# Expert ranks by triangular products, and expert 0's first products written into the last attention blocks

## The chip, the cores and the metric

The kernel runs on one core of one Trainium2 chip. The metric is the time of one execution on the device in microseconds; three executions are known, and a fourth was profiled. TensorE (PE) multiplies; VectorE (DVE), ScalarE (ACT) and GpSimd (POOL) do the elementwise work; SyncE (SP) issues the loads, GpSimd the scatters.

## The reference

A sliding-window attention with sink tokens is followed by a mixture of experts with a sticky top-1 gate. Four batches, 8 heads, 768 positions, head size 64; 8 experts, 512 to 1024 to 512.

```python
scores = q @ k.T / sqrt(D)                     # keep: key < n_sink (4) or 0 <= row - col < window (128)
a = softmax(where(keep, scores, -1e9)); x = (a @ v), heads side by side      # [B, S, 512]
for s in range(S):                             # the sticky gate, per batch
    fresh_e = argmax(x[b, s] @ w_gate)
    e = fresh_e if s == 0 or sigmoid(x[b, s] @ w_local) < 0.5 else prev_e
    prev_e = e
    out[b, s] = softmax(logits)[e] * (relu(x[b, s] @ w1[e]) @ w2[e])
```

## The kernel before

All products are in float32 made of two reduced parts: a high part h, a low part l, and the three products h·h, h·l, l·h.

**Attention.** 8 groups (4 batches, two halves of the heads) of 6 blocks of 128 rows: 48 blocks, in the loop `for n in range(nb + 3)` in `attention`. It is a pipeline written out by hand: iteration n issues the scores of block n (`score`, L548), turns block n-1 (`turn`, L578, copied by ScalarE at L585), applies block n-2 to v (`apply`, L609 and L614, into tile av), and finishes block n-3 (`collect` L500, `back` L504 into bank bk, `finish` L520 and L524). The mask step L560 on VectorE makes the row maximum and ScalarE takes the exponential (L563). Each engine works through its own list in this order; a wait at one instruction holds all that stand behind it on that engine. Tiles of tag "b" (bk, and the small PSUM tiles of the routing) share one bank.

**Routing.** When the last block of a batch is finished, `routing` is put on a list, and `step()` runs one piece of it per iteration, as the tables STEPS and ENDING say. A piece reduces the gate logits (L248), finds the expert (L252 to L266, ends with fk: fresh expert, and whether the token sticks), turns fk on PE (`turn`, L280, tile tf), and runs the sticky gate along the tokens as a scan on VectorE over 8 partitions (`stay`, L285). Then `count` finds a token's rank among those of its expert: a second scan (L291, running counts ct, carried from batch to batch in `run`) and a product (L293), per half of 384 tokens. PE brings expert, slot base and rank back to rows (tile tm, L326, `base_r`), VectorE makes slots and chances (L332 to L339), and GpSimd scatters the token rows into the buffer xs at their slots (L342), one transfer per block.

**Between.** The last batch is routed in two parts, blocks 0 to 2 (`LAST`) in the branch, blocks 3 to 5 after it. Meanwhile ScalarE and GpSimd split expert 0's first weights into w_a (`first_high` L446, `first_low` L450), and two blocks of rows of expert 0 that earlier batches have scattered are read back and turned (`early_rows`, `early_prep`, tile xpfe).

**Experts.** After the branch a planner (`Agenda`, with due times by estimated product time) mixes `ffn` of expert 0's early 256 rows (first products L1000 into h_s, second products L1049 into the two `late` banks), the tail's routing, `counts`, the loads of the next rows (`lead`, xrsn, L934), and the split of w_b (expert 0's second weights, L879 by ScalarE, L880 by VectorE or GpSimd). Then each expert runs an arm of a switch, chosen by its number of rows (`tc.Switch`); `between` issues the late second products while the switch jumps. In expert 0's arm (the rest of its rows, 64 at a time of 128 columns in this data: L991) four chunks of expert 1's first weights are split into w_c, as SHORT says: ScalarE casts (L879), GpSimd or VectorE subtracts (L880).

Of the kernel before, what the change touches and what calls it, by code (L numbers as in the profile page):

```python
# [43 lines left out]
MERGE = 7  # L44
WARM = 12
# [12 lines left out]
NSM = NBLK * E + NBLK + B * NBLK + 10  # L58
# [8 lines left out]
def kernel(ctx, tc, qkd, vn, vs, w1, w2, nw, c_misc, c_ident, c_idw, c_small,  # L67
# [12 lines left out]
    xs = dram.tile([E * CAP, ROW], F32, name="xs")  # L80

# [149 lines left out]
    base_r = rt.tile([40, 10], F32R, name="base_r")

    def setup():
        nc.sync.dma_start(xs[0:P, :], zrow)
        nc.gpsimd.tensor_copy(identb, ident)
        nc.scalar.copy(base_r, base_f)

    def routing(b, i0, i1, sfx, ps, ptag, apart=False):
        n = f"{sfx}{b}_{i0}"
        nb, q0, q1 = i1 - i0, i0 * P, i1 * P  # L240
        nq = nb * P
        xb, lw, orr = xb_t[b % 2], lw_t[b % 2], orr_t[b % 2]

        def tile(nm, *shape, dt=F32, bufs=1):
            return rt.tile([P, NBLK, *shape], dt, tag=nm, bufs=bufs, name=f"{nm}{n}")[:, 0:nb]
# [3 lines left out]
        if apart:  # L249
            yield  # L250
# [6 lines left out]
        nc.vector.tensor_reduce(out=m2, in_=eq, axis=AX.X, op=ALU.max)  # L257
        nc.vector.scalar_tensor_tensor(out=fr, in0=lg[:, :, E], scalar=-1.5 * 2.0 ** -23,
                                       in1=first[:, i0:i1], op0=ALU.is_lt, op1=ALU.max)
        if apart:  # L260
            yield
        fk = fk_t[:, 0:nb]
# [4 lines left out]
        if not apart:  # L267
            yield
# [32 lines left out]
        if apart:  # L301
            chances()
# [996 lines left out]
```

## Time and profile before

| what | us |
|---|---|
| three runs | 599.86, 602.12 (median), 609.26 |
| the profiled execution: time, span | 606.81, 605.0 |
| first scores to last scores (47 blocks) | 5.98 to 224.78 |
| last scores to expert 0's arm | 224.78 to 284.39 |
| expert 0's arm | 284.39 to 304.86 |
| experts 1 to 7 | 313.31 to 605.0 |

Mean granted TensorE clock 0.925. A row of the order of time has start, length, engine, line, operation, output<-inputs, shapes and count, and in brackets the idle time before it and what ended it. A row by stretches has start:end and length, then for each of the five engines its busy time and count, then the granted clock, the share of the DMA engines and GB/s.

### The profile page before, as it was taken

The page shows a single profiled execution, that of the slowest core. Times are in us where ns is not written, and L with a number is a line of the kernel's source. Part 1 is how long each engine was busy: PE and PEld are TensorE (multiplying, and loading weights), DVE is VectorE, ACT ScalarE, POOL GpSimd, SP SyncE. Part 2 cuts the span into 40 slices and gives each one's busy share as a digit, 9 for nine tenths or more (in the row PEclk, how much of TensorE's full clock was granted, in tenths as well). Part 3 has the DMA queues.
Part 4 walks back from the last instruction along what each step waited for, and adds up shares of the span by engine and source line. Part 5 has one row for each costly group of instructions (what it writes and reads, how often), then busy time and mean ns, then how long its engine had stood idle before and what let it go on. Part 6 is the DMA issues. An engine that isn't in the chain of part 4 may idle for free. (4 is left out here: it accounts for less than half of the span.)

```text
span 605.0 us, 11792 instructions
## 1 busy us (share of the span) xinstructions
PE 541.8 (90%) x3896; PEld 458.8 (76%) x3896; DVE 354.4 (59%) x1288; ACT 284.9 (47%) x850; POOL 233.3 (39%) x188
## 2 busy tenths in 40 slices
PE   6899997989788886779589999989999899999995
PEld 3688786768667765668579978887887679888894
DVE  5677887587758865563736627464454866272321
ACT  2788785578548574222426318161532636132220
POOL 4973370837181064132616106253440355302201
PEclk7699998899799898579679999999999999999999
DMA  8633403252234034138148027484632719211000
GB/s 298 254 105 127 168 12 157 89 186 91 74 137 162 1 117 164 59 106 260 62 117 284 37 74 262 142 282 126 255 122 64 264 66 343 77 39 38 36 22 34
DMA packets 30473, 80.38 MB, mean 133 GB/s; under 512 B 3774, under 2 KB 5310, under 8 KB 30272
## 3 DMA queue, kind: packets, MB, share of 16 engines
q1 hardware_dynamic: 25520, 65.41, 31.4%
q0 software_dynamic: 4176, 12.64, 5.5%
q14 instruction: 148, 1.21, 0.7%
q8 instruction: 53, 0.87, 0.7%
q10 hardware_dynamic: 576, 0.25, 0.1%
HBM read 63.27 MB, written 16.06 MB: 131 GB/s over the span
## 5 line engine op out<-in xcount | busy, mean ns | idle before, releaser
L563 ACT ACTIVATE pef<-smf,biasf 128x264 f32<-128x264 f32 (+2 forms) x192 | 93.6, 489 | 58.8 <-DVE biasf L560 58.8
L560 DVE CUSTOM_DVE_ANT_0 smf<-sf,mask 128x264 f32<-128x264 f32 (+2 forms) x192 | 66.8, 402 | 14.6 <-PE sf L548 7.9
L1011 ACT ACTIVATE hx<-h 128x256 fp32r<-128x256 f32 (+3 forms) x72 | 24.2, 359 | 107.4 <-PE h L1000 91.7
L1049 PE MATMUL late<-w_a,hx 128*128 128x512 f32 (+2 forms) x288 | 68.8, 393 | 1.0 <-issue 1.0
L979 DVE SCALAR_TENSOR_TENSOR hx<-h,hx 128x256 fp32r<-128x256 f32 (+3 forms) x72 | 26.7, 390 | 70.2 <-ACT hx L1011 66.1
L1049 PEld LDWEIGHTS late<-w_a,hx 128*128 128x128 f32 (+2 forms) x288 | 50.7, 179 | 14.5 <-issue 1.5
L578 PE MATMUL tpf<-ident,pef 128*128 128x128 f32 x352 | 56.3, 300 | 2.2 <-ACT ptf L585 2.0
L1049 PE MATMUL late<-w_b,hx 128*128 128x512 f32 (+1 forms) x216 | 55.7, 415 | 2.3 <-DMA xs<-zrun 2.0
L1031 POOL DMA_INDIRECT out_dram<-ot_d,oi_d x18 | 18.7, 1037 | 100.4 <-DVE ot_d L1030 80.2
L614 PE MATMUL avf<-ptf,v 128*64 128x128 f32 x704 | 54.1, 294 | 1.6 <-issue 1.6
L1049 PEld LDWEIGHTS late<-w_b,hx 128*128 128x128 f32 (+1 forms) x216 | 41.6, 196 | 14.0 <-ACT w_b L879 2.1
L585 ACT COPY ptf<-tpf 128x512 f32<-128x512 f32 (+1 forms) x96 | 51.1, 532 | 1.0 <-issue 0.5
L578 PEld LDWEIGHTS tpf<-ident,pef 128*128 128x128 f32 x352 | 40.9, 150 | 12.4 <-ACT ptf L585 5.4
L1011 ACT ACTIVATE hx<-hs 128x96 fp32r<-128x96 f32 (+2 forms) x72 | 16.7, 274 | 70.6 <-DVE hs L994 59.5
L614 PEld LDWEIGHTS avf<-ptf,v 128*64 128x64 f32 x704 | 40.7, 145 | 7.7 <-issue 3.2
L520 DVE TENSOR_TENSOR xb<-bkf,rsf 128x256 f32<-128x256 f32 x48 | 20.3, 423 | 36.4 <-ACT ptsf L595 28.1
L504 PE MATMUL bkf<-idw,xtf 128*128 128x146 f32 x192 | 35.8, 311 | 5.2 <-DVE xtf L500 2.3
L880 POOL TENSOR_TENSOR w_c<-raw,w_c 128x1024 fp32r<-128x1024 f32 x11 | 27.9, 2543 | 31.6 <-ACT w_c L879 26.2
L342 POOL DMA_INDIRECT xs<-xb,slotf x21 | 20.5, 976 | 50.9 <-DVE early_i L362 31.8
L880 POOL TENSOR_TENSOR w_b<-raw,w_b 128x1024 fp32r<-128x1024 f32 x10 | 25.6, 2556 | 36.3 <-ACT w_b L879 27.8
L880 POOL TENSOR_TENSOR w_a<-raw,w_a 128x1024 fp32r<-128x1024 f32 x10 | 26.5, 2650 | 30.2 <-ACT w_a L879 28.1
L548 PE MATMUL sf<-w_a 64*128 64x264 f32 (+2 forms) x288 | 29.2, 325 | 8.3 <-DVE biasf L560 2.2
(228 smaller groups left out, 1146.2 us busy)
## 6 DMA issues: line engine op xcount, KB each, us to landing
raw<-in_dram SPq DMA_DIRECT2D x53, 512.0 KB, 6.0
raw<-in_dram SPq DMA_DIRECT2D x14, 800.0 KB
xr_0n<-xs SPq DMA_DIRECT2D x21, 258.0 KB, 2.7
v<-in_dram SPq DMA_DIRECT2D x7, 768.0 KB, 8.4
raw_w<-in_dram SPq DMA_DIRECT2D x7, 512.0 KB
raw<-in_dram SPq DMA_DIRECT2D x10, 256.0 KB
xs<-zrun SPq DMA_DIRECT2D x9, 258.0 KB
xr_0r<-xs SPq DMA_DIRECT2D x8, 258.0 KB, 3.1
```

Source lines behind the costliest of these rows:

```text
L342: s_i = nc.gpsimd.indirect_dma_start(out=xs[:, :], out_offset=bass.IndirectOffsetOnAxis(ap=slot[:, j:j + 1].bitcast(U32), axis=0), in_=xb[ ...
L504: mm = nc.tensor.matmul(bk[:, pr * WX:(pr + 1) * WX], blk["xt"][:, pr, :], idw[:, g * NPR + pr, :], start=True, stop=True, skip_group_chec ...
L548: u["mm"] = nc.tensor.matmul(sps[:, t, :w], qx[ROWS[t], i * P:(i + 1) * P], kx[ROWS[t], off:off + w], start=m == 0, stop=m == 2)
L560: u["dve"] = nc.vector.tensor_tensor_reduce(out=sm[:, :w], in0=sps[:, t, :w], in1=mk, scale=-0.125, scalar=BIG, op0=ALU.add, op1=ALU.min, ...
L563: nc.scalar.activation(pe[:, h, :w], sm[:, :w], AF.Exp, bias=bias[:, t:t + 1], scale=-1.0, accum_out=z[:, h, 0:1])
L578: nc.tensor.transpose(tp[:, t, k, :], pe[:, 2 * c + t, o:o + P], ident)
L585: nc.scalar.copy(pt[:, :, 0:nt, :], tp[:, :, 0:nt, :])
L614: nc.tensor.matmul(avt[ROWS[t], pr, :], prep["v"][:, j, 2 * pr + t, :], x["pt"][:, t, k, :], start=i < 2 and pr == 0 and k == 0, stop=pr = ...
L880: todo += [lambda s=s: lo(out=l[:, s], in0=raw[:, s], in1=h.bitcast(F32)[:, s], op=ALU.subtract) for s in ([slice(0, FF)] if eng[1] == "po ...
L979: nc.vector.scalar_tensor_tensor(out=d[:, :, 1, :], in0=h, scalar=0.0, in1=d.bitcast(F32)[:, :, 0, :], op0=ALU.max, op1=ALU.subtract)
L1011: relu = nc.scalar.activation(d[:, :, 0, :], h, AF.Relu)
L1049: nc.tensor.matmul(o, a, w, start=t == 0, stop=t == len(mm) - 1, skip_group_check=half)
```

## The change

**Ranks.** The count scans (L291, L293) and `run` go. The experts of all tokens stay as one-hot rows in `ohs` (bf16, made by ScalarE from tm), with the sum over earlier blocks in `cum`. A token's slot is now three kinds of products in one PSUM tile rk: a strictly upper triangle times its own block, ones times the blocks ahead of it in the batch, ones times `cum`, and the slot base. The steps have other tables: pieces 2 and 3 run in one iteration, the second half's scan gets an iteration of its own, tm comes at iteration 9 of 12, rk at 10, slots and scatters at 11.

TensorE, in the fourth group of the loop, around the selection of the first batch; sf are scores, tpf turns, bkf back, avf apply. Before:

```order
L578 MATMUL tpf_1_3_1_1728<-ident,pef_1_3_0_1625 128x128 x4
L589 MATMUL bkf_1733<-ident,pkf_1713 96x128
L504 MATMUL bkf_1733<-idw,xtf_1715 128x146 x2
L609 MATMUL avf_1755<-ptsf_1668,srf_1_1401 128x128 x2
L614 MATMUL avf_1755<-ptf_1_2_0_1666,v_80 64x128 x4
L614 MATMUL avf_1755<-ptf_1_2_1_1676,v_80 64x128 x4
L326 MATMUL tmf_0_1769<-base_r,orr_151 128x10 x6
L548 MATMUL sf_1_5_0_1780<-qk_b 128x264 x6
```

Now:

```order
L670 MATMUL avf_1695<-ptf_1_1_1_1621,v_85 64x128 x4
L321 MATMUL tmf_0_1704<-base_r,orr_155 128x8 x6
L604 MATMUL sf_1_4_0_1719<-hq 128x264 x6
...
L670 MATMUL avf_1776<-ptf_1_2_1_1687,v_85 64x128 x4
L336 LDWEIGHTS identb
L336 MATMUL rkf_0_1787<-ohs,identb 128x48
L336 LDWEIGHTS onesb
L336 MATMUL rkf_0_1787<-cum,onesb 128x48
L336 MATMUL rkf_0_1787<-base_r 128x48
L336 LDWEIGHTS onesb
L336 MATMUL rkf_0_1787<-ohs,onesb 128x40
```

The selection moved one iteration ahead, and eight rank products (five with ohs and ones, the last three not shown) stand behind the next apply, ahead of the scores of block 5. (The triangle's tile shares a buffer with identb, whose name the row shows.)

**The last blocks.** The loop ends after 48 iterations. What was iterations 48 to 50, the routing of the last batch (both parts), the counts and the eight first products of expert 0's early rows (`early_first`, 12 products each, into four two-bank tiles and the banks a and b) is written out in one list. `first_high` and `first_low` run an iteration earlier, and first for the half of the columns that the first four products read. TensorE's list from the turn of block 47 on, before:

```order
L578 MATMUL tpf_1_5_1_3682<-ident,pef_1_5_0_3596 128x128 x4
L589 MATMUL bkf_3687<-ident,pkf_3673 96x128
L504 MATMUL bkf_3687<-idw,xtf_3675 128x146 x2
...
L280 MATMUL tff_0_0_3733<-identb,fk 8x128
L504 MATMUL bkf_3743<-idw,xtf_3741 128x146 x2
...
L504 MATMUL bkf_3762<-idw,xtf_3760 128x146 x2
L326 MATMUL tmf_0_3770<-base_r,orr_152 128x10 x3
L384 MATMUL xpfe_3789<-ident,xr_164 128x128 x4
L384 MATMUL xpfe_3798<-ident,xr_165 128x128 x4
L834 UNCONDITIONAL_BRANCH
```

Now (he are expert 0's first products):

```order
L634 MATMUL tpf_1_5_1_3735<-ident,pef_1_5_0_3637 128x128 x4
...
L449 MATMUL hef_3782<-x_a,w_a 128x256 x12
...
L560 MATMUL bkf_2_3814<-idw,xtf_1_3810 128x146 x2
L449 MATMUL hef_3782<-x_a,w_a 128x256 x12
...
L449 MATMUL hef_3849<-x_a,w_a 128x256 x12
L321 MATMUL tmf_0_3873<-base_r,orr_156 128x8 x3
L449 MATMUL hef_3849<-x_a,w_a 128x256 x12
...
L449 MATMUL hef_3986<-x_a,w_a 128x256 x12
L449 MATMUL hef_4002<-x_a,w_a 128x256 x24
L985 UNCONDITIONAL_BRANCH
```

The rows of expert 0 are turned ahead of block 47, the first products fill the list between the small steps of the routing, and none is left behind the branch.

**After the branch.** No planner: 8 casts of w_b by ScalarE, 8 subtractions by VectorE, the 32 products with high weights (both late banks in turn, f by f), the rows' turns, then the 16 with low weights. Two chunks of expert 1's first weights are split here, the other two in expert 0's arm, both by GpSimd. VectorE in that arm, before and now (64 rows):

```order
L994 TENSOR_REDUCE hs_1_0_1_11625<-h_1_0_1_11616 128x64
L979 SCALAR_TENSOR_TENSOR hx<-hs_1_0_0_11610,hx 128x64
L880 TENSOR_TENSOR w_c<-raw,w_c 128x512 x2
L994 TENSOR_REDUCE hs_1_0_2_11652<-h_1_0_2_11643 128x64
L979 SCALAR_TENSOR_TENSOR hx<-hs_1_0_1_11625,hx 128x64
```
```order
L1114 TENSOR_REDUCE hs_1_0_1_11875<-h_1_0_1_11866 128x64
L1099 SCALAR_TENSOR_TENSOR hq<-hs_1_0_0_11860,hq 128x64
L1114 TENSOR_REDUCE hs_1_0_2_11896<-h_1_0_2_11887 128x64
L1099 SCALAR_TENSOR_TENSOR hq<-hs_1_0_1_11875,hq 128x64
L1145 COPY oi_1_d_11901<-xm_61 128x1
```

VectorE has no subtraction of weights there any more. The tile hx lies now where the keys of the odd groups lay (hq).

The diff, cut to its core:

```diff
-STEPS = {2: 1, 3: 1, 4: 1, 5: 1, 9: 1, 10: 1, 11: 2}
-ENDING = {38: 1, 39: 1, 40: 1, 41: 1, 42: 1, 43: 1, 44: 2, 45: 1, 47: 1, 48: 2, 49: 1, 50: 2}
+STEPS = {2: 1, 3: 2, 4: 1, 5: 1, 9: 1, 10: 1, 11: 2}
+ENDING = {38: 1, 39: 2, 40: 1, 41: 1, 42: 1, 43: 1, 44: 2, 45: 1, 46: 2}
-FIRST = 0, 2, 1, 3, 4, 6, 5, 7
+FIRST = 0, 2, 4, 6, 1, 3, 5, 7
...
-        def count(h):
-            w, c = len(parts[h]) * P, h * hb * P
-            o = oh[:, q0 + c:q0 + c + w]
-            nc.vector.tensor_tensor_scan(ct[:, c:c + w], ones8.broadcast_to([E, w]), o, ct[:, c - 1:c] if c else run,
-                                         ALU.mult, ALU.add)
-            nc.vector.tensor_tensor(out=orr[32:40, q0 + c:q0 + c + w], in0=ct[:, c:c + w], in1=o, op=ALU.mult)
...
+        tm = ps.tile([P, NBLK, E], F32, tag=ptag, name=f"tm{n}")[:, 0:nb]
         for j in range(nb):
+            nc.tensor.matmul(tm[:, j, :], orr[:, q0 + j * P:q0 + (j + 1) * P], eye_r, start=True, stop=True)
+        oh_k = ohs[:, k0:k0 + nb]
+        nc.scalar.copy(oh_k, tm)
...
+        rk = ps.tile([P, NBLK, E], F32, tag=ptag, name=f"rk{n}")[:, 0:nb]
+        mm = [(rk, trib, oh_k), (rk, onesb, cum.unsqueeze(1).broadcast_to([P, nb, E])),
+              (rk, ones_r, cap_r.unsqueeze(1).broadcast_to([E, nb, E]))]
+        for j in range(nb - 1):
+            mm.append((rk[:, j + 1:nb], onesb, oh_k[:, j:j + 1].broadcast_to([P, nb - 1 - j, E])))
+        for x, (o, w, m) in enumerate(mm):
+            nc.tensor.matmul(o, w, m, start=x == 0, stop=x == len(mm) - 1, skip_group_check=True)
...
+    def early_first(f, hs):
+        h1, l1 = w1_of(0)
+        mm = [(w, a, k) for k in range(KC) for w, a in ((h1, 0), (h1, 1), (l1, 0))]
+        for t, (w, a, k) in enumerate(mm):
+            nc.tensor.matmul(hs, w[:, k, f * P:(f + 1) * P], early_x[0][:, k, a, :n_e], start=t == 0,
+                             stop=t == len(mm) - 1)
+        d = hx[:, f, 0:2 * n_e].rearrange("p (j a c) -> p j a c", a=2, c=P)
+        nc.scalar.activation(d[:, :, 0, :], h, AF.Relu)
...
-                for n in range(nb + 3):
+                for n in range(nb):
...
+                apply(z, f"{nm}_0")
+                collect(z[0]["blk"], f"{nm}_0")
+                next(head_r)
+                next(head_r)
+                first_steps(0)
+                apply(a, f"{nm}_1")
...
+                next(tail_r)
+                first_steps(3)
...
+                low_steps(2)
+                counts(ps_t, "t")
...
+                first_steps(5)
+                low_steps(2)
+                first_steps(6, 7)
+                low_steps(4)
...
+    with tc.manual_schedule(engines=set(ORDERED)):
         for c in range(3):
             w_load(NCH + c)
+        for c in range(KC):
+            h, l = h2(2 * c, 2), l2(2 * c, 2)
+            second_high(second_raw[c], h)
+            for s in halves:
+                last_low = nc.vector.tensor_tensor(out=l[:, s], in0=second_raw[c][:, s], in1=h.bitcast(F32)[:, s],
+                                                   op=ALU.subtract)
+        for f in range(FC):
+            for j in (1, 0):
+                for a in range(2):
+                    late_product(f, j, a, h2, start=f + a == 0)
...
-    SHORT = (("act", "pool"), ("act", "dve"), ("act", "pool"), ("act", "pool"))
+    SHORT = (("act", "pool"),)
...
+    for c in range(2):
+        h, l = [t[:, c, :] for t in w1_of(1)]
+        second_high(raw_t[c], h)
+        i = nc.gpsimd.tensor_tensor(out=l, in0=raw_t[c], in1=h.bitcast(F32), op=ALU.subtract)
...
+    for j in range(2):
+        preps[j][0]()
+    for f in range(FC):
+        late_product(f, 1, 0, l2, stop=f == FC - 1)
+    for j in range(2):
+        preps[j][1]()
+    preps[2][0]()
+    for f in range(FC):
+        late_product(f, 0, 0, l2, stop=f == FC - 1)
+    preps[2][1]()
+    store_late(1, "_0")
```

More of the change, by code (lines that the diff above doesn't have):

```diff
@@ L57 @@
 MISC = N2 + SK
[L58 removed]
+NBASE = 2 * E + P
+NSM = NBLK * E + NBLK + B * NBLK + NBASE + P
 NX = HG * SK * 3
@@ L301, in routing @@
-        if apart:
-            chances()
-        turn(0)
-        if apart:
-            yield
-        for h in range(1, len(parts)):
-            turn(h)
-            stay(h - 1)
-            if apart:
-                yield
-        if not apart:
-            chances()
-            yield
-        stay(len(parts) - 1)
-        if not apart:
-            yield
-        for h in range(len(parts)):
-            if apart and h == len(parts) - 1:
-                yield
-            count(h)
-        nc.vector.tensor_copy(run, ct[:, nq - 1:nq])
@@ new lines, in routing @@
+        if not direct:
+            rp, rk = rk, tile("rks", E)
+            nc.scalar.copy(rk, rp)
+        yield
+        slot = tile("slot", dt=I32, bufs=2)
+        sl = tile("sl", E)
+        nc.vector.tensor_tensor(out=sl, in0=rk, in1=oh_k, op=ALU.mult)
+        nc.vector.tensor_tensor(out=ex, in0=ex, in1=oh_k, op=ALU.mult)
+        with nc.allow_low_precision(reason="one of eight summands is not zero, an integer below 2^15"):
+            nc.vector.tensor_reduce(out=slot, in_=sl, axis=AX.X, op=ALU.add)
@@ L801, in attention, with bank, ending @@
                     step()
-                for _ in early_prep(sfx, ps_s, "s"):
-                    pass
+                y, z, a = blocks[nb - 3:]
+                b, g = B - 1, G - 1
+                nm = f"{sfx}{nb}"
+                def bank(k):
+                    return ps_t.tile([P, 512], F32, tag="t", name=f"bk{nm}_{k}")
+                def ending(blk, i, bk):
+                    finish(b, g, i, blk, bk, nm)
+                (high0, low0), (high1, low1) = early_prep(sfx, ps_s, "s")
@@ new lines, in attention @@
+                bk = bank(1)
+                back(g, z[0]["blk"], bk)
+                collect(a[0]["blk"], f"{nm}_1")
+                ending(z[0]["blk"], NBLK - 2, bk)
+                bk = bank(2)
+                back(g, a[0]["blk"], bk)
+                next(head_r)
+                ending(a[0]["blk"], NBLK - 1, bk)
+                next(tail_r)
+                first_steps(1)
+                next(head_r)
+                first_steps(2)
+                next(head_r)
+                next(tail_r)
@@ L823, in attention @@
                 free.append(True)
-                pend.append(early_prep(sfx, ps_s, "s"))
+                while pend:
+                    step()
                 first_load(range(2 * KC))
@@ L830, in attention @@
                     second_load(c)
-            while pend:
-                step()
+                for high, low in early_prep(sfx, ps_s, "s"):
+                    high()
+                    low()
+                counts(ps_m, m_tag)
+                masked()
+                for f in range(FC):
+                    early_first(f, ps_s.tile([P, 2, 512], F32, tag="s", name=f"he{sfx}{f}")[:, 0, 0:n_e])()
     with tc.If(narrow != 0) as branch:
```

344 lines of the change are left out of this document (197 added, 147 removed).

## The prediction

> **What bounds the kernel now.** I read the summary first (PE busy 90% of the span, every other engine under 60%), then cut the span by the groups of the attention loop, then read TensorE's order of time wherever a stretch was longer than its like. These are busy times by stretch; the times at the left are the first scores of groups 1 to 7, then the last scores, the end of the branch, expert 0's arm, and experts 1 to 7.
>
> ```profile
> core 0: us, PE busy (x) PEld busy (x) DVE busy (x) ACT busy (x) POOL busy (x), PEclk, DMA share, GB/s
> 35.21:56.57 21.36, 21.36 (x242) 18.56 (x241) 16.50 (x86) 17.73 (x65) 11.86 (x11) 1.00 0.32 120
> 56.57:81.46 24.89, 22.89 (x255) 19.24 (x253) 20.19 (x101) 20.43 (x71) 11.93 (x11) 1.00 0.27 103
> 81.46:111.45 29.99, 26.93 (x248) 23.12 (x246) 22.40 (x94) 19.29 (x67) 13.51 (x12) 0.83 0.23 86
> 111.45:139.39 27.94, 24.10 (x255) 19.47 (x253) 20.42 (x104) 19.26 (x67) 15.84 (x18) 1.00 0.41 149
> 139.39:169.39 30.00, 26.79 (x248) 23.02 (x246) 22.43 (x94) 19.37 (x67) 13.51 (x12) 0.83 0.26 87
> 169.39:198.02 28.63, 24.37 (x255) 19.64 (x253) 20.24 (x104) 19.06 (x66) 11.94 (x14) 1.00 0.42 154
> 198.02:224.78 26.76, 22.71 (x206) 18.61 (x205) 18.24 (x84) 16.16 (x54) 7.32 (x8) 0.87 0.16 61
> 224.78:248.57 23.79, 14.85 (x120) 12.01 (x118) 14.72 (x64) 10.75 (x30) 10.82 (x10) 0.76 0.39 127
> 248.57:284.39 35.82, 31.95 (x169) 27.67 (x170) 17.32 (x63) 9.31 (x21) 9.36 (x6) 0.83 0.44 145
> 284.39:304.86 20.47, 13.13 (x77) 11.85 (x77) 15.39 (x33) 7.78 (x20) 9.69 (x5) 0.68 0.27 88
> 313.31:605.00 291.69, 277.39 (x1624) 240.12 (x1624) 143.47 (x369) 106.06 (x267) 92.96 (x52) 0.99 0.39 134
> ```
>
> Group 1, without routing, takes 21.36 us and PE is always busy: the loop is PE's at full clock. The others are 3.5 to 8.6 us longer, and groups 3 and 5, where tokens are counted, run at a mean clock of 0.83. From the last scores to expert 0's arm (59.6 us) PE is busy 46.8 us at clocks of 0.76 and 0.83, and in expert 0's arm 13.1 of 20.5 us at 0.68. Experts 1 to 7 (291.7 us) have PE busy at 0.99, and the change hardly touches them. So three stretches can give something.
>
> **Ranks in the loop.** In group 3 the counting step stands on VectorE ahead of work that PE needs. TensorE (groups 2 and 3; tff is the same kind of step where nothing is counted), then VectorE, then the clock (the third number from the right):
>
> ```profile
> 76.69 0.54 PE L280 MATMUL tff<-identb,fk 128*8 128x128 bf16 x6 [1.63 <-ACT ptf L585]
> ...
> 81.03 0.50 PE L280 MATMUL tff<-identb,fk 128*8 128x128 bf16 x6
> ...
> 94.32 1.09 PE L614 MATMUL avf<-ptf,v 128*64 128x128 f32 x16
> ...
> 99.24 0.28 PE L589 MATMUL bkf<-ident,pkf 128*96 128x128 f32 x1 [1.71 <-DVE pkf L568]
> ...
> 104.34 0.37 PE L326 MATMUL tmf<-base_r,orr 40*128 40x10 f32 x1 [0.82 <-DVE orr L293]
> ```
> ```profile
> 95.94 0.28 DVE L599 TENSOR_TENSOR ptsf<-bkf,ptsf 32x128 fp32r<-32x128 f32 x1
> 96.35 0.97 DVE L285 TENSOR_TENSOR_SCAN orr<-kff,orr 8x384 fp32r<-8x384 bf16 x1
> 97.25 0.98 DVE L291 TENSOR_TENSOR_SCAN ctf<-ones,zrun,orr 8x384 f32<-8x384 f32 x1
> 98.27 0.55 DVE L293 TENSOR_TENSOR orr<-ctf,orr 8x384 fp32r<-8x384 f32 x1
> ```
> ```profile
> 101.00:110.00 9.00, 7.73 (x48) 6.90 (x44) 4.76 (x19) 4.32 (x17) 4.08 (x4) 0.50 0.00 0
> 261.55:264.26 2.71, 2.71 (x14) 2.71 (x14) 1.94 (x16) 0.10 (x1) 1.40 (x2) 0.50 0.06 23
> ```
>
> Each half of a batch costs a count scan and a product, 0.98 + 0.55 = 1.5 us of VectorE, once ahead of pkf (PE waits 1.71) and once ahead of tm (PE waits 0.82 for the fourth of six products). Then the clock is at 0.50 for nine microseconds. All of this goes. In its place the selection products (tm) stand an iteration later than the last scan, so that wait is gone, and eight rank products (rk) stand an iteration after these. Both write bank b, which VectorE gives free with the last reader of bk, L599 in this fence: it ends at 96.22, PE's apply at 95.41. I charge each of the two stops this lag, 0.8, and its products. The trace has no rank products: 0.083 each as tff (0.50 for 6 bf16 products at full clock) is the lower bound, 0.37 as tm at half clock the upper; eight are 0.7 to 3.0. I take 0.9, since they are bf16 with small outputs as tff. So two stops are 3.5; with 1.4 for the new reductions and the scan left over, groups 3 and 5 come to 21.4 + 4.9 = 26.3: **−3.7 each**. Groups 2, 4 and 6 get the second scan (0.97) that stood in the next group, **+0.9 each**; steps 2 and 3 now follow each other in one iteration: the wait of 1.63 for fk grows by step 2's five small ops to some 2.6, and pkf is no longer delayed by these an iteration before, no difference. In group 7 the counting goes, but three small products of expert 0's row count and flags wait there: **−1.4**. Sum −7.4 + 2.7 − 1.4 = **−6**; from −12 (all stops hidden) to +8 (three more clock drops at 4.5, below).
>
> **The last blocks and the branch's end.** TensorE again, and what two of its products cost at full clock:
>
> ```profile
> 228.17 1.09 PE L614 MATMUL avf<-ptf,v 128*64 128x128 f32 x16
> ...
> 235.00 0.53 PE L280 MATMUL tff<-identb,fk 128*8 128x128 bf16 x6 [1.44 <-DVE fk L265]
> ...
> 243.32 0.77 PE L326 MATMUL tmf<-base_r,orr 40*128 40x10 f32 x3 [2.21 <-DVE orr L293]
> ...
> 248.57 5.46 PE L1000 MATMUL h_s<-x_a,w_a 128*128 128x256 f32 x24 [2.57 <-issue]
> ...
> 260.65 0.49 PE L326 MATMUL tms<-base_r,orr 40*128 40x10 f32 x3 [1.66 <-DVE orr L293]
> ...
> 281.51 1.03 PE L384 MATMUL xpsn<-ident,xrsn 128*128 128x128 f32 x8
> ...
> 313.31 11.54 PE L1000 MATMUL h<-x_a,w_c 128*128 128x256 f32 x96 [0.59 <-DMA out_dram<-ot_d,oi_d]
> ...
> 328.26 8.46 PE L1049 MATMUL late<-w_a,hx 128*128 128x512 f32 x36
> ```
>
> PE ends block 45's apply at 229.3 and then walks from wait to wait. The changed list puts expert 0's 96 products (11.54 in group 313.31, at full clock) into these waits. From 229.3: 16 transposes 2.1; the two applies left, 16 products in 1.09 and two sink products, 2.6; three banks of sink and back products at about 0.4, an estimate from the same row, 1.3; 96 products 11.5; 12 tff 1.0; 20 small ones (tm, rk, counts) at 0.1, 2.0; waits that stay (the last exponentials, both scans; an estimate) 1.7: 22.2, so PE leaves the branch at 251.5. VectorE keeps up: its list there is shorter by the two count scans. The jump costs 2.6 (the 2.57 of issue), the first cast of w_b 0.6 (no PE work covers it). Then 32 high products at 8.46/36 = 0.235 are 7.5, 1.7 more because a gap of 3.2 will have halved the clock; 12 transposes 1.5; 16 low products 3.8; 0.5 for a bank of x_b: 270.1 against 284.4, **−14.3**. The lower bound of the gain is −8: the lows run on VectorE now, and rows can come late. These are POOL's and SP's rows:
>
> ```profile
> 265.11 0.96 POOL L342 DMA_INDIRECT xs<-xb,slots  x1 [0.30 <-issue]
> 269.06 1.79 SPq L934 DMA_DIRECT2D xrsn<-xs x3
> xrsn<-xs SPq DMA_DIRECT2D x3, 258.0 KB, 4.4
> ```
>
> SP's loads start 3.0 after the last scatter and land 4.4 later. The tail's rank products stand ahead of expert 0's last three (3 × 12 products, 4.3, before 251.5); with the counts on VectorE between, the slots come at about 249, three scatters (0.96, some 0.3 apart) end at 253, rows are there at 260 to 262, and PE wants them at 263.8: just hidden; SP has only the pad and weight loads ahead of them. The upper bound is −20 (no halved clock, no waits).
>
> **Expert 0's arm.** VectorE, then ScalarE and GpSimd:
>
> ```profile
> 291.11 3.45 DVE L880 TENSOR_TENSOR w_c<-raw,w_c 128x512 fp32r<-128x512 f32 x2 [1.73 <-ACT w_c L879]
> 294.69 2.17 DVE L979 SCALAR_TENSOR_TENSOR hx<-hs,hx 128x64 fp32r<-128x64 f32 x1
> 298.22 3.13 DVE L979 SCALAR_TENSOR_TENSOR hx<-hs,hx 128x64 fp32r<-128x64 f32 x1
> 301.67 0.21 DVE L979 SCALAR_TENSOR_TENSOR hx<-hs,hx 128x64 fp32r<-128x64 f32 x1
> ```
> ```profile
> 290.48 3.20 ACT L879 CAST w_c<-raw 128x512 fp32r<-128x512 f32 x6
> 291.50 5.28 POOL L880 TENSOR_TENSOR w_c<-raw,w_c 128x1024 fp32r<-128x1024 f32 x2 [3.71 <-ACT w_c L879]
> ```
>
> Four chunks of expert 1's weights are split inside this short arm, and VectorE's ops stretch whenever GpSimd splits (2.17 and 3.13 for one that takes 0.21). Two chunks move ahead of the arm, under the late products, and the two that stay go to GpSimd: VectorE loses 3.45, ScalarE four of its casts, 4 × 3.20/6 = 2.1. I keep both stretched ops: **−5.6**; from −9 (they go too) to 0. [...]
>
> **Sum.** −6.0 − 14.3 − 5.6 = −25.9. The profiled execution has a span of 605.0 and a time of 606.8: 579.1 and 580.9. It is 4.7 above the median of the runs shown, 602.1; predicted for the median is **576 us**.
>
> **Rivals.** (1) Expert 0's arm is GpSimd's. Its two chunks (2.6 each) start only when ScalarE has cast them, the rows come late, and the arm keeps its 20.5 while the end of the branch gives 10: 602 − 6 − 10 = 586. For it: GpSimd is the last to finish in that arm now; against: one chunk fewer and none on VectorE. (2) More than I count: the two products hide in VectorE's lag, the clock stays whole, and the stretched ops go: −12 − 18 − 9, 563. (3) **The slower side**: the clock. PE now stops at fk, tm and rk in three batches and at two small products in group 7: 11 places. A drop costs what 101 to 110 shows, 9 us at half clock, about 4.5. A gap of 1.63 (76.69) did not drop the clock, 1.66 (260.65) did at once, the 0.50 of 261.55. My stops of 0.8 to 2.6 lie around that. With four drops beyond those counted the time is 576 + 18 = 594; from six it is slower than before, and with nine, 616. Against it: before, groups 2, 4 and 6 show a whole clock in spite of such waits. [...] (4) That the ranks' new form does not shorten the loop at all is the case of 0 for the first term, 582, inside my forecast.
>
> **Chances.** The forecast, 569 to 584: 0.58. Rival 1, 586: 0.17, a quarter of it above the 2% line. Rival 2, 563: 0.10. Rival 3: 0.10 at about 594, 0.05 at 616. What a measurement of this kernel can tell from no change is about 2%, 12 us: faster lies under 590. Faster 0.58 + 0.13 + 0.10 = 0.81, same 0.04 + 0.10 = 0.14, slower 0.05. The range 562 to 592 leaves out rival 3 and part of rival 2.
>
> **What would show it.** Right: groups 3 and 5 near 26 us at a clock of 1.0; no count scans; 96 products of expert 0 ending some 26 us after the last scores; a gap of about 3 at the branch's end; first product of expert 0's arm 45 us after the last scores, that arm 14 to 15 us. Wrong: clocks of 0.8 in groups 2 to 6; PE waiting for rows ahead of the low products; an arm of 20.

## The result, and the profile after

The changed kernel takes **579.9 us** (median of four runs, 579.1 to 584.0) against 603.6 of the kernel before in the same comparison (599.9 to 609.3): a ratio of 0.964, 95% interval 0.957 to 0.972. Forecast were 576 and 562 to 592. On three more chips the same two kernels gave 0.984 (0.979 to 0.989), 0.969 (0.960 to 0.977) and 0.968 (0.962 to 0.975). The second chip is the odd one, and the experiments come back to it.

The stretches of the first profile of the changed kernel (two groups and the late product inside the arm left out), cut at the same events as those of before: the first scores of groups 2 to 7, the last scores, the first late product, expert 0's arm, the late product inside it, and experts 1 to 7.

```profile
core 0: us, PE busy (x) PEld busy (x) DVE busy (x) ACT busy (x) POOL busy (x), PEclk, DMA share, GB/s
58.23:84.41 26.18, 23.58 (x255) 20.39 (x254) 20.16 (x99) 20.49 (x71) 11.44 (x11) 0.93 0.26 98
84.41:110.25 25.84, 24.55 (x256) 21.42 (x254) 19.05 (x94) 18.91 (x68) 11.60 (x11) 0.93 0.26 99
110.25:138.47 28.22, 24.13 (x254) 20.72 (x252) 22.16 (x102) 19.68 (x68) 17.73 (x19) 0.94 0.44 147
...
192.27:216.89 24.62, 21.09 (x217) 18.35 (x216) 18.63 (x94) 19.12 (x65) 11.18 (x11) 0.93 0.17 66
216.89:247.40 30.51, 25.46 (x237) 23.07 (x237) 19.83 (x95) 12.23 (x35) 10.41 (x10) 1.00 0.43 151
247.40:261.57 14.17, 14.17 (x61) 11.48 (x61) 7.71 (x19) 7.26 (x14) 4.73 (x2) 0.88 0.78 230
261.57:275.47 13.90, 9.43 (x78) 8.71 (x76) 10.22 (x30) 5.45 (x15) 6.68 (x4) 0.89 0.54 159
...
282.79:578.30 295.51, 280.09 (x1625) 241.14 (x1624) 145.42 (x369) 106.19 (x267) 92.97 (x52) 0.99 0.39 133
```

Groups 3 and 5 are 26 us long, not 30, at a clock of 0.93, not 0.83. From the last scores to expert 0's arm there are 44.7 us, not 59.6, and TensorE is at full clock up to the branch's end (1.00 in the row of 216.89). The same cuts in two pairs of traces (the second pair, named before again and third below, comes from one chip):

| stretch (us) | before | changed | before again | changed, third | forecast of the difference |
|---|---|---|---|---|---|
| start to group 1 | 35.2 | 36.9 | 35.0 | 36.6 | 0 |
| group 1 | 21.4 | 21.3 | 21.4 | 21.3 | 0 |
| groups 2, 4, 6 | 81.5 | 82.3 | 78.7 | 80.6 | +2.7 |
| groups 3, 5 | 60.0 | 51.7 | 59.7 | 50.2 | -7.4 |
| group 7 | 26.8 | 24.6 | 24.4 | 23.9 | -1.4 |
| last scores to expert 0's arm | 59.6 | 44.7 | 60.6 | 44.7 | -14.3 |
| expert 0's arm and its late products | 28.9 | 21.2 | 27.7 | 21.0 | -5.6 |
| experts 1 to 7 | 291.7 | 295.5 | 293.6 | 295.2 | 0 |
| span | 605.0 | 578.3 | 601.0 | 573.6 | -25.9 |

TensorE in groups 2 to 4 of the changed kernel (start, duration, line, product, in brackets the idle time ahead and its releaser):

```profile
74.56 0.80 PE L298 MATMUL tff<-identb,fk 128*8 128x128 bf16 x6 [2.50 <-DVE fk L280]
...
99.83 0.80 PE L321 MATMUL tmf<-base_r,orr 8*128 8x8 f32 x6 [0.96 <-ACT pef L619]
...
105.92 0.20 PE L336 MATMUL rkf<-ohs,identb 128*128 128x48 bf16 x1
...
106.28 0.28 PE L336 MATMUL rkf<-ohs,onesb 128*128 128x40 bf16 x5
106.50 1.00 PE L604 MATMUL sf<-hq 64*128 64x264 f32 x12
...
128.44 0.50 PE L298 MATMUL tff<-identb,fk 128*8 128x128 bf16 x6 [3.95 <-DVE fk L280]
```

The wait for the flags (fk) in group 2 is 2.50, that for the selection products (tm) 0.96. The profile puts the end of this second wait, at 99.83, down to ScalarE's exponential (pef); VectorE's last reader of the bank ends at 99.68, so which of the two held the products is not shown. The eight rank products (rk) do not wait at all and take 0.58 together, 105.92 to 106.50. In group 4 the wait for the flags is 3.95. VectorE and GpSimd there, in this order:

```profile
125.56 0.17 DVE L267 TENSOR_REDUCE mxf<-lgf 128x6 f32<-128x48 f32 x1
125.77 1.10 DVE L270 TENSOR_TENSOR eqf<-lgf,mxf 128x48 f32<-128x48 f32 x1
126.90 0.76 DVE L271 TENSOR_TENSOR eqf<-eqf,small 128x48 f32<-128x48 f32 x1
```
```profile
124.94 1.86 POOL L134 TENSOR_TENSOR hq<-raw,hq 128x800 fp32r<-128x800 f32 x1
126.88 0.71 POOL L549 TENSOR_TENSOR srf<-sxf,srf 32x256 fp32r<-32x256 f32 x1
```

Two VectorE ops of 0.21 each (that is what they take in group 2, at 73.33 and 73.57) last 1.10 and 0.76 here; they end at 126.87 and 127.66, and GpSimd's two subtractions at 126.80 and 127.59.

The end of the branch on TensorE, and ScalarE's two rows around the jump:

```profile
224.35 1.67 PE L449 MATMUL hef<-x_a,w_a 128*128 128x256 f32 x12
...
237.90 3.04 PE L449 MATMUL hef<-x_a,w_a 128*128 128x256 f32 x24
241.42 1.68 PE L449 MATMUL hef<-x_a,w_a 128*128 128x256 f32 x12 [0.47 <-ACT hq L453]
247.40 9.26 PE L1229 MATMUL late<-w_b,hq 128*128 128x512 f32 x32 [4.30 <-ACT w_b L1226]
256.50 1.03 PE L425 MATMUL xpsn<-ident,xrsn 128*128 128x128 f32 x8
```
```profile
243.14 0.38 ACT L453 ACTIVATE hq<-hef 128x256 fp32r<-128x256 f32 x1 [1.77 <-PE hef L449]
246.66 4.26 ACT L1226 CAST w_b<-raw 128x512 fp32r<-128x512 f32 x8 [3.14 <-PEq L1258]
```

TensorE ends expert 0's early products at 243.1, 26.2 after the last scores (forecast 26.7). The gap is 4.30: ScalarE's last rectifier ends at 243.52, and the stop around the jump (3.14, which the row puts down to TensorE's sequencer at L1258, the load of the arm's register) and the first cast follow one another. The 32 high products take 9.26 at a mean clock of 0.82, with 0.50 from 249 to 251 (forecast 9.2, half clock included). The rows' turns at 256.50 wait for nothing.

### The profile page after: what moved, and what is told of

It reads as the page before. It is cut to its first block, busy times and chain, and to the rows that moved or that the text cites. A ratio compares the mean times of both kernels' runs of the same rounds, so it can differ in the third digit from the quotient of the medians.

```text
span 578.3 us, 11794 instructions
## 1 busy us (share of the span) xinstructions
PE 526.2 (91%) x3933; PEld 451.0 (78%) x3933; DVE 343.4 (59%) x1270; ACT 285.0 (49%) x854; POOL 228.2 (39%) x191
## 5 line engine op out<-in xcount | busy, mean ns | idle before, releaser
L1131 ACT ACTIVATE hq<-h 128x256 fp32r<-128x256 f32 (+3 forms) x72 | 24.2, 360 | 110.4 <-PE h L1120 94.7
L1169 PE MATMUL late<-w_a,hq 128*128 128x512 f32 (+2 forms) x288 | 70.2, 398 | 1.2 <-issue 1.2
L1099 DVE SCALAR_TENSOR_TENSOR hq<-h,hq 128x256 fp32r<-128x256 f32 (+3 forms) x72 | 26.6, 390 | 68.6 <-ACT hq L1131 67.1
L1169 PEld LDWEIGHTS late<-w_a,hq 128*128 128x128 f32 (+2 forms) x288 | 50.8, 179 | 15.8 <-issue 1.7
L1131 ACT ACTIVATE hq<-hs 128x96 fp32r<-128x96 f32 (+2 forms) x72 | 16.7, 273 | 68.2 <-DVE hs L1114 61.0
L670 PE MATMUL avf<-ptf,v 128*64 128x128 f32 x704 | 50.2, 284 | 0.0
L1169 PE MATMUL late<-w_b,hq 128*128 128x512 f32 (+1 forms) x168 | 42.1, 409 | 0.8 <-ACT x_a L428 0.8
L1169 PEld LDWEIGHTS late<-w_b,hq 128*128 128x128 f32 (+1 forms) x168 | 32.0, 192 | 9.5 <-ACT x_a L428 1.2
L1029 POOL TENSOR_TENSOR w_a<-raw,w_a 128x1024 fp32r<-128x1024 f32 x10 | 26.5, 2652 | 27.7 <-ACT w_a L1028 25.5
L619 ACT ACTIVATION_READ_ACCUMULATOR pef<-smf,biasf 128x1 f32 x192 | 36.3, 189 | 0.0
L1120 PEld LDWEIGHTS h<-x_a,w_c 128*128 128x128 f32 x288 | 34.3, 188 | 0.7 <-issue 0.6
```

The costliest lines, as they stand in the source:

```text
L619: nc.scalar.activation(pe[:, h, :w], sm[:, :w], AF.Exp, bias=bias[:, t:t + 1], scale=-1.0, accum_out=z[:, h, 0:1])
L670: nc.tensor.matmul(avt[ROWS[t], pr, :], prep["v"][:, j, 2 * pr + t, :], x["pt"][:, t, k, :], start=i < 2 and pr == 0 and k == 0, stop=pr = ...
L1029: todo += [lambda s=s: lo(out=l[:, s], in0=raw[:, s], in1=h.bitcast(F32)[:, s], op=ALU.subtract) for s in ([slice(0, FF)] if eng[1] == "po ...
L1099: nc.vector.scalar_tensor_tensor(out=d[:, :, 1, :], in0=h, scalar=0.0, in1=d.bitcast(F32)[:, :, 0, :], op0=ALU.max, op1=ALU.subtract)
L1120: nc.tensor.matmul(hs, w[:, k, fs], x, start=t == 0, stop=t == len(mm) - 1)
L1131: relu = nc.scalar.activation(d[:, :, 0, :], h, AF.Relu)
```

## The experiments

Each was run with repeated timing beside the kernel before on its chip. First chip: the comparison above; second chip: the first four; third chip: the next four; fourth chip: the last four. Medians of the kernel before: 607.0, 600.6 and 599.7.

### The changed kernel again, three times

No edit. First time, on the second chip:

> The changed kernel once more, as it is. In its first profile the loop up to the last scores was 9.6 us shorter than before (my sum said 6), the last blocks with the branch's end 14.9 (14.3), expert 0's arm with its late products 7.7 (5.6 for the arm), but the start was 1.7 longer and experts 1 to 7 were 3.8 longer, which I had at nothing. If these two losses belong to the changed program, they stand in this profile again, within 0.5 us each. Rival: they are the scatter of single executions; then this profile has them at other sizes, under 1 us or of the other sign. The time: 22 to 26 us under the kernel before in either case.

595.9 us against 607.0: 11 us, not the 22 to 26 that I expected in either case. The start is again longer (36.4 against 35.0 to 35.2), so this belongs to the program; experts 1 to 7 take 294.5. The loop is another than in the first trace: groups 2, 4, 6 take 90.8, and the stretch to the first late product 36.4. TensorE in group 4, and VectorE:

```profile
116.18 0.77 PE L560 MATMUL bkf<-idw,xtf 128*128 128x146 f32 x4 [0.80 <-issue]
...
119.97 0.39 PE L604 MATMUL sf<-w_a 64*128 64x264 f32 x2 [1.03 <-issue]
120.93 0.79 PE L604 MATMUL sf<-w_a 64*128 64x264 f32 x6 [0.57 <-DVE biasf L616]
```
```profile
120.09 0.42 DVE L616 CUSTOM_DVE_ANT_0 smf<-sf,mask 128x256 f32<-128x256 f32 x1 [2.18 <-remote]
```

Two engines stop here at once, and no wait of the program explains it (issue, remote). The first trace of the kernel before has the same stops at the same place, 0.83, 0.35 and 0.43; the first of the changed kernel has none. So the first pair of traces was not under one condition, and I sent both kernels to one chip.

> The kernel before once more, as it is, beside the changed one on the same chip. On a second chip the changed kernel was only 11 us under the kernel before (595.9 to 607.0) where the first showed 24, and its trace there has stops of TensorE that no wait explains (named issue: 1.83, 1.24 and 1.31 us in groups 4, 6 and 7, a lower clock behind each) and that its first trace has not; the first trace of the kernel before has them (1.61, 1.29, 1.19). Theory A: these stops come at the row scatters and hit either kernel by chance of the chip; then on a chip where the changed kernel has them the kernel before has them too and the gain is 20 or more in the median of chips, or where both lack them. Theory B: the kernel before always has them, and the changed one has them on some chips only, so the gain is 24 where it lacks them and 11 where it has them. The time: 600 to 610.

> The changed kernel a third time. If the stops named issue in groups 4, 6 and 7 stand in its trace, 592 to 598; if not, 578 to 585. Its stage table beside that of the kernel before on this chip tells what the change gives where both are under the same condition: by the theory of the prediction 8 to 10 in the loop and 13 to 16 from the last scores to expert 0's arm; by theory B of the run before this, 0 to 2 in the loop when the stops stand in both.

602.1 and 580.6 us, and both traces lack the stops: this is the fair pair of the table. The loop is 8.1 shorter, last scores to arm 15.9, the arm 6.7; the start loses 1.6 and experts 1 to 7 lose 1.6. The two profiled executions took 602.8 and 575.4, and the second is the fastest of its four, so the table's 27.4 is more than the medians' 20 to 22. Neither theory A nor B is needed on this chip. What stays of them: the gain is 20 to 24 us on three chips and 11 on the second, where the changed kernel, the ranks alone and two variants all show the stops in groups 4, 6 and 7. In the changed kernel's trace there TensorE also stands 3.69 us at the end of the branch where it stands 0.47 in the others. No trace of the kernel before was taken on that chip. In the first trace of the kernel before and in the second of the changed kernel the stops lie beside the six row scatters of a batch or within 2 us of them (in group 7 the last scatter ends at 223.21 and 220.47, the last stop at 224.38 and 221.77); what causes them was not tried and stays open.

> The changed kernel once more, as the measure for the three others on the same chip. 575 to 584 and from the last scores to the first late product 30.5, if TensorE's stops named issue are absent from groups 4, 6 and 7; 592 to 598 and 36, if they are there.

579.0 us; no such stops; 30.65 from the last scores to the first late product, as in the first (30.51) and the third trace (30.52).

### The ranks alone

The kernel before with the new `routing` in all places, and its own last blocks, branch end, late products and arm:

```diff
-ENDING = {38: 1, 39: 1, ... 47: 1, 48: 2, 49: 1, 50: 2}
+ENDING = {38: 1, 39: 2, ... 46: 2, 47: 2, 48: 2, 49: 2, 50: 2}
-        for t in (0.0, 1.4, 2.0, 3.0, 6.0, 6.1):
+        for t in (0.0, 0.7, 1.4, 2.0, 3.0, 4.5, 5.5, 6.0, 6.1):
             ag.add(t, route)
```

> The kernel before with the new ranks alone: its own last blocks, branch end, order of late products and arm. My theory: the loop's gain is the ranks' and does not hang on the tail, so 8 to 11 us up to the last scores as in the changed kernel, and another 1 to 3 behind them, since the count scans of the last batch go too: 10 to 13 us under the kernel before. Rival one, that the ranks only move stops about and the tail brings it all: within 3 us of the kernel before. Rival two, the clock: more stops of TensorE at a whole clock cost what the scans gave, so groups 3 and 5 stay near 30 us.

> The new ranks alone, a second time, since in its first run TensorE had stops named issue in groups 4, 6 and 7 (1.78, 1.20 and 2.01 us) that the traces of the kernel before and of the changed one on another chip lack. If those stops are absent here: the loop as in the changed kernel's third trace, 154.7 from group 2's first scores to the last scores against 162.8 before, and the tail as before, less 1 to 3 for the count scans: 7 to 11 us under the kernel before; the remaining 12 to 16 of the change are then the tail's. If they are present: 0 to 4 under it, as in the first run. Rival: even without those stops the ranks give nothing by themselves, within 3 us.

605.7 against 607.0 on the second chip (ratio 0.997, 0.993 to 1.001), 601.4 against 599.7 on the fourth (1.001, 0.998 to 1.004): **no gain**. The rivals that said within 3 us held, and my 10 to 13 and 7 to 11 failed, though in the second of these traces the loop from group 2 to the last scores takes 152.3, against 162.8 in the trace of before again. I had the loop right and the total wrong. TensorE in the last blocks and at the arm of that run:

```profile
221.22 0.42 PE L590 MATMUL bkf<-ident,pkf 128*96 128x128 f32 x1 [3.66 <-DVE pkf L569]
...
228.30 1.31 PE L505 MATMUL bkf<-idw,xtf 128*128 128x146 f32 x4 [2.41 <-DVE xtf L501]
...
276.84 8.77 PE L994 MATMUL h<-x_b,w_a 128*128 128x128 f32 x40 [5.22 <-issue]
```

The new ranks have more pieces, each handed on between TensorE, ScalarE and VectorE. In the old tail pkf waits 3.66 for VectorE, yet other waits are gone: from the last scores to the first late product TensorE is idle 14.0 us, against 14.2 in before again. The stretch is longer by busy time, 31.67 against 28.78 (before again, then this run):

```profile
219.14:262.16 43.02, 28.78 (x215) 25.12 (x213) 27.80 (x104) 17.17 (x45) 19.23 (x16) 0.79 0.35 118
210.99:256.71 45.72, 31.67 (x226) 27.76 (x225) 25.94 (x101) 17.32 (x47) 18.01 (x15) 0.78 0.31 106
```

The arm starts 20.1 after the first late product, not 17.6, behind a stop of 5.22 that no wait explains. And the start is 2.4 longer. GpSimd there, in this run:

```profile
15.72 1.83 POOL L121 CAST qk_b<-raw 128x800 fp32r<-128x800 f32 x2 [0.43 <-DMA raw<-in_dram]
17.52 1.33 POOL L126 TENSOR_TENSOR w_a<-raw,w_a 128x544 fp32r<-128x544 f32 x1
```

Its casts for the second group stand ahead of the first group's low parts, an order that the last section of the experiments comes back to. So the longer start comes with the ranks and not with the last blocks. Of the loop's 10.5 us the start takes 2.4, the tail 2.7, the way to the arm 2.5 and experts 1 to 7 1.5, while the arm with its late products is 2.3 shorter. That leaves 3.7 between two traces from two chips, and nothing between the medians on one chip. The places of the pieces in that tail are mine, so this is the price of one placement, not a bound. That the loop's gain reaches the end only with a tail that covers the pieces is argued, not shown: no run has the new tail without the new ranks.

### Expert 0's early products at the end of the branch

The same work, but all in one piece behind the last blocks' steps:

```diff
-                first_steps(0)
...
-                first_steps(5)
-                low_steps(2)
+                first_steps(0, 1, 2, 3, 4, 5)
+                low_steps(4)
                 first_steps(6, 7)
```

> The changed kernel with expert 0's 96 early products in one piece at the end of the branch and not between the last blocks' steps; nothing else is moved, the low parts follow them. My theory: their 11.5 us lie in waits of TensorE (for exponentials, flags, both scans, the selection and rank products), so the waits come back: 7 to 11 us over the changed kernel, with half clock between. Rival: what gives the 14.9 us is only that counts, slots and rows come sooner, and the products would fit as well behind them: within 3 us of the changed kernel.

> The changed kernel with expert 0's 96 early products in one piece at the end of the branch, a second time. In its first run the stretch from the last scores to the first late product was 39.7 us against 36.4 of the changed kernel on that chip, where both were disturbed; on the other chip the changed kernel has 30.5 in four traces. My theory by the waits of TensorE: 37 to 41 here, 6 to 10 us over the changed kernel. Theory after the first run: the wait for the casts at the end of the branch and for a smaller part of the waits only, 33 to 35, 3 to 4 us over it.

Second chip: 597.7 against 595.9, which is inside the rival's 3 us, and 39.7 to 36.4 in the stretch, with the stops in both traces. Fourth chip: **591.9 against 579.0**, and 39.3 against 30.65. The pair without the stops decides for the first theory. TensorE of the second run:

```profile
230.73 0.49 PE L321 MATMUL tmf<-base_r,orr 8*128 8x8 f32 x3 [1.53 <-DVE orr L307]
...
234.88 0.80 PE L321 MATMUL tmf<-base_r,orr 8*128 8x8 f32 x3 [1.59 <-DVE orr L307]
...
236.64 2.91 PE L449 MATMUL hef<-x_a,w_a 128*128 128x256 f32 x12
240.02 3.84 PE L449 MATMUL hef<-x_a,w_a 128*128 128x256 f32 x24 [0.47 <-ACT hq L453]
```
```profile
217.27:256.59 39.32, 28.59 (x237) 25.73 (x237) 20.06 (x95) 12.61 (x36) 10.46 (x10) 0.85 0.37 125
```

The same products are there (237 matmuls as in the changed kernel's 30.51). The waits for both scans are back, and the clock is 0.85, not 0.97 to 1.00: 12 early products take 2.91 where they take 1.67 at 224.35 above. Of the 8.7 us, busy time is 3.1 (28.59 less 25.48 in the fourth trace), the rest is idle. The spans of the two traces differ by 11.8 us: 1.0 more lies in the loop and 2.7 in experts 1 to 7, which the edit does not touch.

### Four chunks split in expert 0's arm

```diff
-    SHORT = (("act", "pool"),)
+    SHORT = (("act", "pool"), ("act", "dve"), ("act", "pool"), ("act", "pool"))
...
-    for c in range(2):
-        h, l = [t[:, c, :] for t in w1_of(1)]
...
-                        w_agenda(ag, e + 1, 0 if e else 2, KC, ...
+                        w_agenda(ag, e + 1, 0, KC, ...
```

> The changed kernel with the four chunks of expert 1's weights split inside expert 0's arm again (GpSimd, VectorE, GpSimd, GpSimd for the low parts, as before) and none ahead of it. My prediction priced this at 5.6 us, bounds 0 to 9: 4 to 7 us over the changed kernel of the same chip, with VectorE's ops in the arm stretched to 2 to 3 us again. Rival: the arm is bound by its rows and its own chain of products, reductions and casts, and ScalarE and VectorE have room: within 2 us.

583.8 against 580.6 of the changed kernel on that chip: 3.3 by the medians, under the 4 to 7 and with runs that overlap (581.3 to 589.7 and 575.4 to 583.1). The stage shows it more clearly: the arm with its late products is 26.0 against 21.0, 4.9 longer. Its VectorE, then its TensorE, and VectorE in the changed kernel's arm (first trace):

```profile
263.04 5.59 DVE L1029 TENSOR_TENSOR w_c<-raw,w_c 128x512 fp32r<-128x512 f32 x2 [1.66 <-ACT w_c L1028]
```
```profile
268.89 1.97 PE L1111 MATMUL h<-x_b,w_a 128*128 128x128 f32 x8 [6.06 <-DVE hs L1114]
```
```profile
268.34 2.20 DVE L1099 SCALAR_TENSOR_TENSOR hq<-hs,hq 128x64 fp32r<-128x64 f32 x1
...
270.85 1.99 DVE L1099 SCALAR_TENSOR_TENSOR hq<-hs,hq 128x64 fp32r<-128x64 f32 x1
```

In the two traces of the kernel before, the arm has this wait too:

```profile
294.82 1.97 PE L991 MATMUL h<-x_b,w_a 128*128 128x128 f32 x8 [5.78 <-DVE hs L994]
```
```profile
288.13 1.97 PE L991 MATMUL h<-x_b,w_a 128*128 128x128 f32 x8 [3.73 <-DVE hs L994]
```

The wait of 5.78 and 3.73 is back as 6.06: a chunk's two low halves on VectorE stand ahead of the reduction that TensorE waits for. They take 5.59 while GpSimd's two take 5.10 from 262.99; in before again, where GpSimd's next (2.71 at 287.38) starts only when VectorE's release it, they take 1.29.

### Late products by turns

High, high, low for each chunk, first the second block's 24, then the first's:

```diff
         for f in range(FC):
-            for j in (1, 0):
-                for a in range(2):
-                    late_product(f, j, a, h2, start=f + a == 0)
+            for x, (a, t) in enumerate(((0, h2), (1, h2), (0, l2))):
+                late_product(f, 1, a, t, start=f + x == 0, stop=f == FC - 1 and x == 2)
```

> The changed kernel with expert 0's late products in the order of before: for each chunk the two high products and then the low one, first the 24 of the second block, then the rows' turns, then the 24 of the first. VectorE's eight low parts take 0.65 each and 24 products take 5.6 us, so TensorE should hardly wait for them: my theory is that the order high parts first is worth 0 to 2 us, and the stage grows by no more. Rival: the low parts come late, one by one behind the casts, TensorE stops at each and the clock halves: 4 to 8 us over the changed kernel of the same chip.

579.7 against 580.6. The late stage is 2.1 longer (16.2 against 14.2), the arm 2.8 shorter (18.2 against 21.0). So this third part of the change, high parts first, is worth nothing that can be measured; the low parts on VectorE keep ahead of TensorE in either order (its one idle time in this stage, 0.96, is for x_b).

### The flags an iteration later

```diff
-STEPS = {2: 1, 3: 2, 4: 1, 5: 1, 9: 1, 10: 1, 11: 2}
+STEPS = {2: 1, 3: 2, 4: 1, 5: 1, 6: 1, 9: 1, 10: 1, 11: 2}
-        if direct:
+        if direct or b < B - 2:
             yield
```

> The changed kernel with TensorE's turn of the flags one iteration behind the iteration in which VectorE makes them, in the first two batches (the third is as it was). There TensorE stood 2.50 and 3.95 us for the flags and ran at half clock for some two or three us behind each. My theory: the stop is VectorE's lag at the end of one iteration; an iteration later the flags are long there: the stops of groups 2 and 4 go, and their clock is whole: 6.5 us of stops and 2 to 4 of clock, less 1 to 2 for the last scan that moves into the next group: 6 to 9 us under the changed kernel. Rival: VectorE is the engine that is behind in these groups, and the next product that waits for it (sink columns, back product) takes over the stop: within 2 us of the changed kernel.

590.6 against 595.9 on the second chip: 5.3, a little under the 6 to 9. The stop went in part: in group 2 the sink columns wait 0.62 and the flags' turn itself still 1.09, instead of 2.51, and the back product of the next group waits 0.89 for xtf. Group 2 is 2.7 shorter and group 3 2.0 longer, groups 4 and 5 together 3.0 shorter. Another 1.8 lie behind the last scores, which the edit does not touch, so not all of the 5.3 is its own.

### Four edits together

The flags as above, the late products by turns, the arm's two chunks on ScalarE and VectorE, and GpSimd's order in the start:

```diff
-    SHORT = (("act", "pool"),)
+    SHORT = (("act", "dve"),)
...
+            if gi == 1 and first_lows:
+                tc.add_manual_dep(i.ins, first_lows[-1].ins.name, mybir.DependencyInfo(
+                    mybir.DependencyClass.NoSync, mybir.DependencyReason.DATA), reason="order of the lows")
```

> The changed kernel with four edits, each in its own stage. One: GpSimd's low parts of the first group's keys ahead of its casts for the second group, as they stood before (in the changed kernel its casts had slipped ahead, TensorE waits 2.02 and 2.55 us for them, and the start is 1.6 us longer in all its traces): start 35.0 instead of 36.6. Two: the flags turned an iteration later in the first two batches: groups 2 and 4 at 24 to 25 and 25 to 26 instead of 24.8 to 26.3 and 27.6 to 28.5, group 3 up to 2 longer. Three: late products by turns, 0 to 1. Four: the low parts of the two chunks in expert 0's arm on VectorE instead of GpSimd: the ops of 2.20 and 1.99 us there fall back to 0.22, two chunks' low parts of 1.3 us come onto VectorE: 1 to 2 under. Sum 4 to 8 us under the changed kernel of the same chip. Rival: each wait is taken over by the next one, within 2 us.

**573.9 against 579.0** on the fourth chip, and 0.958 (0.952 to 0.964) of the kernel before: the fastest that I ran. By stage: the start 34.0 against 36.8, groups 2 and 3 together 49.7 against 52.2, groups 4 and 5 52.5 against 52.2, late stage and arm 36.3 against 37.1. Only the start is beyond what the unedited kernel shows from trace to trace: its third trace has 49.2 in groups 2 and 3. So these traces do not show that the flags' edit gains anything, and the late products and the arm are inside that scatter too. In group 4 the rival holds: pkf waits 2.56 there in the flags' place, since two of VectorE's ops still take 1.61 and 0.76 beside GpSimd's subtractions. The start is GpSimd's alone. Its rows in the third trace of the changed kernel, and in before again:

```profile
14.99 1.62 POOL L129 CAST hq<-raw 128x800 fp32r<-128x800 f32 x2 [0.70 <-DMA raw<-in_dram]
16.57 1.53 POOL L134 TENSOR_TENSOR w_a<-raw,w_a 128x544 fp32r<-128x544 f32 x1
18.05 1.88 POOL L134 TENSOR_TENSOR hq<-raw,hq 128x800 fp32r<-128x800 f32 x1
19.90 1.78 POOL L134 TENSOR_TENSOR w_a<-raw,w_a 128x544 fp32r<-128x544 f32 x1
```
```profile
13.97 1.67 POOL L125 TENSOR_TENSOR w_a<-raw,w_a 128x544 fp32r<-128x544 f32 x1
15.59 1.83 POOL L120 CAST qk_b<-raw 128x800 fp32r<-128x800 f32 x2
17.39 1.33 POOL L125 TENSOR_TENSOR w_a<-raw,w_a 128x544 fp32r<-128x544 f32 x1
```

GpSimd's order is not written by hand here. With the change, and with the ranks alone, its casts for the second group slipped ahead of the first group's low parts, which TensorE waits for (2.02 and 2.55 us in the first trace). Put back in order, the start is even shorter than before (34.0 against 35.0 and 35.2).

## Why the prediction was right, point by point

- **Ranks in the loop: place and sign right, the size too small.** Forecast -6, measured -9.6 and -8.1. The step that failed is the charge for the rank products, a stop of 0.8 and 0.9 of work in each group: they stand a whole iteration behind the selection products, wait for nothing and take 0.58. That is 1.1 too much in groups 3 and 5 each, and in the pair from one chip the two groups are together 2.1 shorter than forecast. The selection products' stop, 0.8 forecast, is 0.96, but the profile names ScalarE for it; only in group 7 (0.81) does it name VectorE's last reader of the bank, as I had it. The clock of 1.0 that I gave as a sign for groups 3 and 5 is in neither in the first trace (0.93) and in one of the two in the three others. The flags' wait, 2.6 forecast, is 2.50 in group 2 but 3.3 to 4.0 in groups 4 and 6, which I had taken as equal; GpSimd's subtractions lie there (124.94 to 127.59 in group 4).
- **Last blocks and branch end: right.** Forecast -14.3, measured -14.9 and -15.9. (The terms of my sum add up to 269.7, not 270.1, so it should have said -14.7.) TensorE's end in the branch was 0.5 us off, the high products 0.1. The gap was 4.30, not 3.2, because the last rectifier stands ahead of the jump on ScalarE (0.4) and the stop there is 3.14, not 2.6. The 1.7 for half clock behind the gap was my estimate, which no run shows on its own; the 32 products took 9.26 where 0.235 each is 7.5. Rows came in time. That the products live in the waits is shown by the run that took them out: 8.7 us in that stretch, of 12.9 in all.
- **Expert 0's arm: right.** Forecast -5.6 for the arm, measured -6.6 and -5.6; with its late products -7.7 and -6.7. Undoing it alone gave back 4.9 of the stage and 3.3 of the median. How the term is made up is less sure: I took 3.45 of it from VectorE's two low halves in one trace, and in before again they take 1.29, yet the arm gives the same 5.6. The two stretched ops, for which I took no gain, stayed: 2.20 and 1.99 where the others take 0.21 to 0.23. Rival 1, an arm bound by GpSimd's chunks and late rows, would have kept 20 us for the arm; it is 13.9.
- **Two losses that are not in the sum.** The start, +1.6 to +1.7, by GpSimd's order, which came with the ranks: the reordered instructions were there to be seen, and I read the lists only where the diff pointed. And experts 1 to 7, +3.8 and +1.6. The fourth trace of the changed kernel has 293.4 there, as before again (293.6), so part of it varies from trace to trace; the cause of the rest stays open, since no single wait carries it.
- **The sum.** -25.9 was forecast; the spans say -26.7 and -27.4, the medians -20 to -24 on three chips. That the sum came so close is in part luck: in the two pairs of traces the three terms gave 6.2 and 4.7 us more than forecast, and the two losses that I had at nothing took 5.5 and 3.3 of it back. For the median I took off the 4.7 us by which the profiled execution lay over the median of three runs; the stops in its trace were not in my account.
- **Rival 3, the clock,** is a part of the truth, not the outcome. Clocks of 0.93 in groups 3 and 5 are drops that cost 1 to 2 us each, not 4.5: in the third trace group 3 takes 24.4 at a clock of 1.00 and group 5 25.8 at 0.93. On the second chip the time is 595.9, near this rival's 594, yet by stops that it does not have.

## What to carry to other kernels

In this kernel a chain of small dependent steps cost what stood beside it, not what it sums to: the new ranks made the loop ten microseconds shorter, and beside the old tail, with a longer start, the kernel by nothing that could be measured; independent products put between the steps of the last blocks gave 8.7 us there. After such a change, read the order of every engine that a scheduler fills by itself, also in stages that the diff does not touch: the cheapest gain left here was an order that had slipped in the start. And compare two traces only under one condition: here stops that no wait explains stood beside a gain of 11 us on one chip, against 20 to 24 on the others.

## What was not expected of the hardware

A stop of the same length was followed by half clock in one execution of this kernel and not in another. TensorE in the third trace of the changed kernel, groups 2 and 3:

```profile
74.26 0.50 PE L298 MATMUL tff<-identb,fk 128*8 128x128 bf16 x6 [2.52 <-DVE fk L280]
74.69 0.99 PE L604 MATMUL sf<-w_a 64*128 64x264 f32 x12
...
98.19 0.80 PE L321 MATMUL tmf<-base_r,orr 8*128 8x8 f32 x6 [0.96 <-ACT pef L619]
...
99.84 1.09 PE L634 MATMUL tpf<-ident,pef 128*128 128x128 f32 x8
```

After 2.52 us of idle time six small products take 0.50 here and the twelve behind them 0.99, the full clock; in the first trace, after 2.50, the six take 0.80 and the twelve 1.69, at a clock of 0.50 from 74.5 to 76. After 0.96 the transposes keep 1.09 here and take 1.88 in the first (at 101.48). Groups 2 and 3 have clocks of 1.00 and take 24.8 and 24.4 us in this trace, 0.93 and 26.2 and 25.8 in the first. In these traces the length of a stop alone did not decide.
